# An RWKV-6 recurrence and a leaky-ReLU feed-forward on one Trainium2 core, rebuilt: tokens on partitions, three K tiles, 128-token blocks, a planned order

## The chip, the cores and the metric

The kernel runs on one core of one Trainium2 chip. The time is device microseconds of that core. The engines are named as in the profile: PE is TensorE's matmul, PEld its weight load, DVE is VectorE, ACT is ScalarE, POOL is GpSimd and SP is SyncE, which here only issues DMAs.

## The reference

Four batches of eight heads, 768 tokens, 48 elements a head; `r`, `k`, `v`, `w` are f32. A recurrence per head gives 384 values a token, and these go through a feed-forward with 2048 hidden units.

```python
for t in range(S):
    cur = np.einsum('bhd,bhe->bhde', u[None] * kt, vt)
    y[:, :, t] = np.einsum('bhd,bhde->bhe', rt, state + cur)
    state = wt[:, :, :, None] * state + np.einsum('bhd,bhe->bhde', kt, vt)
...
x = attn_out.transpose(0, 2, 1, 3).reshape(B * S, H * D)     # 3072 x 384
h = x @ w_in                                                 # 384 x 2048
g = np.maximum(0.01 * h, h)
out = g @ w_out                                              # 2048 x 384
```

The kernels do the recurrence in chunks of 128 tokens. Within a chunk the decays are products of `w`, so their logarithms are summed with a triangular matmul. `r` and `k` are multiplied by the exponentials of these sums, a masked 128 x 128 score matrix times `v` gives what tokens of one chunk give each other, a 48 x 48 state carries the rest from chunk to chunk, and `r*u*k` summed over a head gives the token's own term.

## The kernel before, in words

It loops over four batches and, in each, over six chunks of 128 tokens; after every third chunk comes a feed-forward block of 384 tokens (`mlp_block`). Only the tile framework orders the work: each engine takes its instructions in the order that the framework's scheduler has given them.

**Loading.** `w` comes as one transfer for a whole batch (L191), and its logarithm is taken in one ACT instruction per batch (L197). `r`, `k` and `v` come by chunk (L212, L216, L220) into f32 tiles with heads padded to 64; POOL clears the padding first (L209 to L211). The feed-forward weights are loaded with a cast to bf16 by POOL's own DMA queue after the first chunk (L127 to L135).

**A chunk.** One matmul gives the suffix sums of the log decays (L227), ACT takes the exponential (L235) and POOL multiplies it with `k` for the state (`dk`, L239). POOL makes `r*u*k` (L241, L245), DVE sums it by head (L249) and scales `v` with it (`vsc`, L251). Then four head pairs: `r` and `k` are transposed in f32 on PE (L261, L269), prefix sums of the decay come transposed from a third matmul (L277), ACT takes their exponentials (L285), DVE multiplies (L290), PE makes two score blocks (L296), DVE masks them (L303). Per head, PE adds the masked scores times `v` (L313), the own term through an identity matmul (L317), the old state's part (L325) and the new state's sum (L332). ACT or DVE copies y, which stands with d_model on partitions, into `xT` (L185), and DVE updates the state (L344). `xT` holds d_model in four K tiles of a head pair each, 112 rows with a gap.

**A feed-forward block.** For each of 16 tiles of 128 hidden units, four matmuls of 384 columns (L149) fill a PSUM tile `hp`, ACT casts it to bf16 (`hs`, L157), and DVE makes max(0.01 h, h) from both (`gt`, L159). Then 3 x 16 matmuls of 384 columns (L171) make three output tiles, copied by ACT (L179) and stored by SP (L180). `hp` and the output tile `op` share two buffers.

Of the kernel before, what the change touches and what calls it, by code (L numbers as in the profile page):

```python
# [8 lines left out]
F32 = mybir.dt.float32  # L9
BF16 = mybir.dt.bfloat16  # L10
AF = mybir.ActivationFunctionType
ALU = mybir.AluOpType
AX = mybir.AxisListType


@with_exitstack
def kernel(
# [11 lines left out]
    nc = tc.nc  # L29
    B, H, S, D = r.shape  # L30
    L = 128
    assert S % L == 0
    C = S // L
    assert H % 2 == 0
    NPAIR = H // 2
    assert D <= 48
    NH = H * D
    NT = NPAIR
    KROWS = 64 + D
    FF = moe_w_in.shape[1]  # L40
    assert FF % 128 == 0
    NFT = FF // 128
    NOUT = moe_w_out.shape[1]
    NTOK = B * S
    MB = 384
    assert S % MB == 0, "sequence must be multiple of mlp block"
    MBC = MB // L

    const = ctx.enter_context(tc.tile_pool(name="const", bufs=1))
    wpool = ctx.enter_context(tc.tile_pool(name="wpool", bufs=1))  # L50
    xtpool = ctx.enter_context(tc.tile_pool(name="xtpool", bufs=1))
    wbpool = ctx.enter_context(tc.tile_pool(name="wbpool", bufs=2))
    natpool = ctx.enter_context(tc.tile_pool(name="natpool", bufs=5))
    slabpool = ctx.enter_context(tc.tile_pool(name="slabpool", bufs=3))
    pairpool = ctx.enter_context(tc.tile_pool(name="pairpool", bufs=8))
    statepool = ctx.enter_context(tc.tile_pool(name="statepool", bufs=2))
    mlppool = ctx.enter_context(tc.tile_pool(name="mlppool", bufs=3))
    gtpool = ctx.enter_context(tc.tile_pool(name="gtpool", bufs=20))
    psum = ctx.enter_context(tc.tile_pool(name="psum", bufs=1, space=bass.MemoryType.PSUM))
    psum2 = ctx.enter_context(tc.tile_pool(name="psum2", bufs=2, space=bass.MemoryType.PSUM))  # L60

    ident_f = const.tile([128, 128], F32, name="ident_f")
    make_identity(nc, ident_f)
    ident_b = const.tile([128, 128], BF16, name="ident_b")
    make_identity(nc, ident_b)

    tcomb = const.tile([128, 256], BF16, name="tcomb")
    nc.gpsimd.memset(tcomb[:, 0:128], 1.0)
    nc.gpsimd.affine_select(
        out=tcomb[:, 0:128],  # L70
        in_=tcomb[:, 0:128],
        compare_op=ALU.is_gt,
        fill=0.0,
        base=0,
        pattern=[[1, 128]],
        channel_multiplier=-1,
    )
    nc.gpsimd.memset(tcomb[:, 128:256], -1.0)
    nc.gpsimd.affine_select(
        out=tcomb[:, 128:256],  # L80
        in_=tcomb[:, 128:256],
        compare_op=ALU.is_ge,
        fill=0.0,
        base=0,
        pattern=[[1, 128]],
        channel_multiplier=-1,
    )
    tsu = const.tile([128, 128], BF16, name="tsu")
    nc.gpsimd.memset(tsu[:], 1.0)
    nc.gpsimd.affine_select(  # L90
        out=tsu[:],
        in_=tsu[:],
        compare_op=ALU.is_gt,
        fill=0.0,
        base=0,
        pattern=[[-1, 128]],
        channel_multiplier=1,
    )
    maskb = const.tile([128, 128], BF16, name="maskb")
    nc.gpsimd.memset(maskb[:], 1.0)  # L100
    nc.gpsimd.affine_select(
        out=maskb[:],
        in_=maskb[:],
        compare_op=ALU.is_gt,
        fill=0.0,
        base=0,
        pattern=[[1, 128]],
        channel_multiplier=-1,
    )
    ukb = const.tile([128, H, D], F32, name="ukb")  # L110
    nc.sync.dma_start(
        out=ukb[:],
        in_=u.rearrange("h d -> (h d)")
        .partition_broadcast(128)
        .rearrange("p (h d) -> p h d", h=H),
    )

    w_in_b = wpool.tile([128, NT, FF], BF16, name="w_in_b")
    w_out_b = wpool.tile([128, NFT, NOUT], BF16, name="w_out_b")
    weights_loaded = [False]  # L120

    def load_weights():
        if weights_loaded[0]:
            return
        weights_loaded[0] = True
        for t in range(NT):
            nc.gpsimd.memset(w_in_b[32:64, t, :], 0.0)  # L127
            nc.gpsimd.dma_start(
                out=w_in_b[0:D, t, :], in_=moe_w_in[(2 * t) * D : (2 * t + 1) * D, :]
            )  # L130
            nc.gpsimd.dma_start(
                out=w_in_b[64 : 64 + D, t, :],
                in_=moe_w_in[(2 * t + 1) * D : (2 * t + 2) * D, :],
            )
        nc.gpsimd.dma_start(  # L135
            out=w_out_b[:], in_=moe_w_out.rearrange("(t p) n -> p t n", p=128)
        )

    xT = xtpool.tile([128, NT, NTOK], BF16, name="xT")

    state_tiles: list = [None] * NPAIR

    def mlp_block(q: int):
        T0 = q * MB
        gts = []
        for j in range(NFT):
            hp = psum2.tile([128, MB], F32, name="hp", tag="hpop")
            for t in range(NT):
                nc.tensor.matmul(  # L149
                    hp[:],  # L150
                    lhsT=w_in_b[0:KROWS, t, j * 128 : (j + 1) * 128],
                    rhs=xT[0:KROWS, t, T0 : T0 + MB],
                    start=(t == 0),
                    stop=(t == NT - 1),
                )
            hs = gtpool.tile([128, MB], BF16, name="hs", tag="hs", bufs=4)
            nc.any.tensor_copy(out=hs[:], in_=hp[:])  # L157
            gt = gtpool.tile([128, MB], BF16, name="gt", tag="gt")
            nc.vector.scalar_tensor_tensor(  # L159
                out=gt[:],  # L160
                in0=hp[:],
                scalar=0.01,
                in1=hs[:],
                op0=ALU.mult,
                op1=ALU.max,
            )
            gts.append(gt)
        for tsub in range(MB // 128):
            op = psum2.tile([128, NOUT], F32, name="op", tag="hpop")
            for j in range(NFT):  # L170
                nc.tensor.matmul(  # L171
                    op[:],
                    lhsT=gts[j][:, tsub * 128 : (tsub + 1) * 128],
                    rhs=w_out_b[:, j, :],
                    start=(j == 0),
                    stop=(j == NFT - 1),
                )
            osb = mlppool.tile([128, NOUT], F32, name="osb", tag="osb")
            nc.any.tensor_copy(out=osb[:], in_=op[:])  # L179
            nc.sync.dma_start(  # L180
                out=out[T0 + tsub * 128 : T0 + (tsub + 1) * 128, :], in_=osb[:]
            )

    def xt_copy(src_ap: bass.AP, p: int, col0: int):
        nc.any.tensor_copy(out=xT[:, p, col0 : col0 + L], in_=src_ap)  # L185

    for b in range(B):
        for p in range(NPAIR):
            state_tiles[p] = None
        w_nat = wbpool.tile([128, H * C, D], F32, name="w_nat", tag="w_nat")  # L190
        nc.sync.dma_start(  # L191
            out=w_nat[:],
            in_=w[b].rearrange("h (c p) d -> p (h c) d", p=128),
        )
        lw = wbpool.tile([128, C, H, 64], BF16, name="lw", tag="lw")
        nc.gpsimd.memset(lw[:, :, :, D:64], 0.0)
        nc.scalar.activation(  # L197
            out=lw[:, :, :, 0:D].rearrange("p c h d -> p h c d"),
            in_=w_nat[:].rearrange("p (h c) d -> p h c d", h=H),
            func=AF.Ln,  # L200
        )
        for c in range(C):
            t0 = c * L
            col0 = b * S + t0
            lw_c = lw[:, c, :, :]
            nat_rf = natpool.tile([128, H, 64], F32, name="nat_rf", tag="nat_rf")
            nat_kf = natpool.tile([128, H, 64], F32, name="nat_kf", tag="nat_kf")
            nat_vf = natpool.tile([128, H, 64], F32, name="nat_vf", tag="nat_vf")
            nc.gpsimd.memset(nat_rf[:, :, D:64], 0.0)  # L209
            nc.gpsimd.memset(nat_kf[:, :, D:64], 0.0)  # L210
            nc.gpsimd.memset(nat_vf[:, :, D:64], 0.0)  # L211
            nc.sync.dma_start(  # L212
                out=nat_rf[:, :, 0:D],
                in_=r[b, :, t0 : t0 + L, :].rearrange("h p d -> p h d"),
            )
            nc.sync.dma_start(  # L216
                out=nat_kf[:, :, 0:D],
                in_=k[b, :, t0 : t0 + L, :].rearrange("h p d -> p h d"),
            )
            nc.sync.dma_start(  # L220
                out=nat_vf[:, :, 0:D],
                in_=v[b, :, t0 : t0 + L, :].rearrange("h p d -> p h d"),
            )
# [129 lines left out]
            if b == 0 and c == 0:  # L353
                load_weights()
# [33 lines left out]
```

## Time and profile before

| | |
|---|---|
| time, median of 2 runs | 391.64 us (390.86 to 392.42) |
| span in the profile | 385.2 us, 6034 instructions |
| HBM read and written | 25.36 MB and 4.72 MB |
| mean granted TensorE clock | 0.978 |
| L149 hp, 512 matmuls, start to start in a run of eight | 162.5 ns |
| L157 ACT cast of hp, 122 | 480 ns mean |
| L159 DVE max, 128 | 554 ns mean |
| L285 ACT exponential of 256 columns, 96 | 384 ns mean |
| L303 DVE mask of 128 columns, 192 | 286 ns mean |
| L241 POOL product of 384 columns, 24 | 1051 ns mean |
| table loads on ACT, 8 | 1283 ns each |

The busy totals say what share of the span an engine had work. In a row of tenths, each digit is a fortieth of the span. Busy times of PE are modelled: a matmul's end lies past the start of the next, so PE's price is best read from starts. A group's idle column says what the engine waited for just before it; an engine that isn't the bound may wait at no cost.

### The profile page before, as it was taken

How to read it: one execution, taken by the hardware profiler on the slowest of the kernel's cores; microseconds unless marked ns; L12 is line 12 of the kernel's file. 1: busy time of each engine (PE TensorE's matmuls, PEld its weight loads, DVE VectorE, ACT ScalarE, POOL GpSimd, SP SyncE). 2: the span in 40 equal slices, each digit the busy share in tenths (PEclk: the TensorE clock that was granted, in tenths of full speed). 3: DMA queues.
4: the chain of work that ended last, by engine and by line, in shares of the span. 5: the costliest groups of instructions: out<-in, count | busy, mean ns of one | idle time of the engine just before them, and what ended most of it. 6: DMA issues, size and time to landing. Idle time of an engine off the chain costs nothing.

```text
span 385.2 us, 6034 instructions
## 1 busy us (share of the span) xinstructions
PE 337.2 (88%) x2136; PEld 187.8 (49%) x2136; DVE 219.8 (57%) x662; ACT 161.4 (42%) x382; POOL 107.8 (28%) x177
## 2 busy tenths in 40 slices
PE   0455169999999999999999999999999999999886
PEld 0232034455555555556555555555555655555343
DVE  0434045448656884767568837675588457724450
ACT  1535012343375633454486433542375235512341
POOL 5893055141152431234144303331331011000000
PEclk9999999999987999999999999999999999998699
DMA  7999999131532225212323233222220100010001
GB/s 159 176 205 227 217 166 167 15 64 20 128 57 54 39 57 115 48 21 53 96 42 58 57 93 60 41 43 82 43 41 3 62 2 0 2 61 3 0 0 63
DMA packets 87295, 27.33 MB, mean 71 GB/s; under 512 B 75489, under 2 KB 86881, under 8 KB 87265
## 3 DMA queue, kind: packets, MB, share of 16 engines
q1 hardware_dynamic: 84688, 23.80, 31.9%
q0 software_dynamic: 2576, 3.15, 4.8%
q8 instruction: 17, 0.28, 0.3%
q14 instruction: 14, 0.11, 0.1%
HBM read 25.36 MB, written 4.72 MB: 78 GB/s over the span
## 4 chain that ended last, share of the span: by engine, by line
PE 79%; SPq 7%; DMA 5%; DVE 5%; ACT 2%; issue 1%
PE hp L149 24%; PE op L171 16%; PE ytsu L325 7%; PE ytsu L332 6%; PE ytsu L313 6%; PE trcs L261 5%; PE mt L296 4%; DMA w_nat<-in_w_dram 4%; SPq L212 4%; PE trcs L269 3%; PE trcs L277 3%; PE ytsu L317 3%; DVE gt L159 2%; SPq L191 2%; PE esu_ps L227 1%; DVE vsc L251 1%
## 5 line engine op out<-in xcount | busy, mean ns | idle before, releaser
L149 PE MATMUL hp<-xT,w_in_b 112*128 112x384 bf16 x512 | 112.5, 347 | 8.6 <-DVE gt L159 7.0
L159 DVE SCALAR_TENSOR_TENSOR gt<-hp,hs 128x384 bf16<-128x384 f32 x128 | 70.1, 554 | 29.6 <-ACT hs L157 28.3
L157 ACT CAST hs<-hp 128x384 bf16<-128x384 f32 x122 | 58.3, 480 | 53.7 <-PE hp L149 52.3
L149 PEld LDWEIGHTS <-w_in_b 112*128 112x128 bf16 x512 | 50.2, 102 | 41.6 <-issue 18.7
L303 DVE TENSOR_TENSOR mtm<-mt,maskb 128x128 bf16<-128x128 f32 x192 | 51.2, 286 | 27.8 <-PE mt L296 27.1
L171 PE MATMUL op<-w_out_b,gt 128*128 128x384 bf16 x384 | 63.7, 326 | 0.4 <-DVE gt L159 0.4
L285 ACT ACTIVATE ef<-trcs 128x256 f32<-128x256 f32 x96 | 36.2, 384 | 47.6 <-PE trcs L277 45.3
L171 PEld LDWEIGHTS <-gt 128*128 128x128 bf16 x384 | 37.6, 98 | 25.0 <-issue 0.6
L313 PE MATMUL ytsu<-mtm,nat_v 128*64 128x128 bf16 x192 | 47.0, 255 | 1.3 <-DVE mtm L303 1.3
L239 POOL TENSOR_TENSOR dk<-nat_kf,esu 128x512 bf16<-128x512 f32 x24 | 27.8, 1157 | 71.7 <-ACT esu L235 71.3
L185 ACT CAST xT<-ytsu 128x128 bf16<-128x128 f32 x88 | 23.4, 266 | 51.0 <-PE ytsu L332 50.3
L261 PE MATMUL trcs<-ident_f,nat_rf 128*128 128x128 f32 x96 | 32.5, 338 | 13.1 <-DMA nat_rf<-in_r_dram 9.7
L317 PE MATMUL ytsu<-ident_b,vsc 128*64 128x128 bf16 x192 | 43.6, 236 | 0.0
L290 DVE TENSOR_TENSOR rka<-trcs,ef 128x256 bf16<-128x256 f32 x96 | 39.0, 408 | 4.7 <-ACT ef L285 4.7
L332 PE MATMUL ytsu<-nat_v,dk 128*64 128x64 bf16 x192 | 40.8, 222 | 0.0
L325 PE MATMUL ytsu<-rka,s_new 64*64 64x128 bf16 x160 | 40.3, 252 | 0.0
L313 PEld LDWEIGHTS <-nat_v 128*64 128x64 bf16 x192 | 20.2, 110 | 36.8 <-issue 28.8
L296 PE MATMUL mt<-rka 48*128 48x128 bf16 x192 | 28.4, 236 | 8.0 <-DVE rka L290 8.0
L241 POOL TENSOR_TENSOR t<-nat_rf,ukb 128x384 f32<-128x384 f32 x24 | 25.2, 1051 | 32.4 <-DMA nat_rf<-in_r_dram 32.3
L179 ACT COPY osb<-op 128x384 f32<-128x384 f32 x24 | 11.5, 479 | 52.5 <-PE op L171 52.5
L344 DVE SCALAR_TENSOR_TENSOR s_new<-s_new,atot,ytsu 128x64 bf16<-128x64 bf16 x80 | 21.9, 277 | 18.8 <-ACT xT L185 18.2
L251 DVE TENSOR_TENSOR vsc<-nat_vf,diag 128x512 bf16<-128x512 f32 x24 | 22.9, 956 | 14.3 <-PE ytsu L317 14.2
(47 smaller groups left out, 323.0 us busy)
## 6 DMA issues: line engine op xcount, KB each, us to landing
nat_rf<-in_r_dram SPq DMA_DIRECT2D x24, 192.0 KB, 3.2
nat_kf<-in_k_dram SPq DMA_DIRECT2D x24, 192.0 KB, 3.6
nat_vf<-in_v_dram SPq DMA_DIRECT2D x24, 192.0 KB, 2.9
out_dram<-osb SPq DMA_DIRECT2D x24, 192.0 KB, 1.9
w_in_b<-in_moe_w_in_dram POOLq DMA_DIRECT2D x8, 192.0 KB, 8.9
w_out_b<-in_moe_w_out_dram POOLq DMA_DIRECT2D x1, 1536.0 KB, 20.6
ukb<-in_u_dram SPq DMA_DIRECT2D x1, 192.0 KB, 3.6
w_nat<-in_w_dram SPq DMA_DIRECT2D x4, 0.2 KB, 16.3
```

Source lines behind the costliest of these rows:

```text
L149: nc.tensor.matmul(hp[:], lhsT=w_in_b[0:KROWS, t, j * 128 : (j + 1) * 128], rhs=xT[0:KROWS, t, T0 : T0 + MB], start=(t == 0), stop=(t == N ...
L157: nc.any.tensor_copy(out=hs[:], in_=hp[:])
L159: nc.vector.scalar_tensor_tensor(out=gt[:], in0=hp[:], scalar=0.01, in1=hs[:], op0=ALU.mult, op1=ALU.max,)
L171: nc.tensor.matmul(op[:], lhsT=gts[j][:, tsub * 128 : (tsub + 1) * 128], rhs=w_out_b[:, j, :], start=(j == 0), stop=(j == NFT - 1),)
L261: nc.tensor.matmul(trcs[:, 0:128], lhsT=nat_rf[:, hA : hA + 2, :].rearrange("p h d -> p (h d)"), rhs=ident_f[:], is_transpose=True, start= ...
L290: nc.vector.tensor_tensor(out=rka[:], in0=trcs[:, 0:256], in1=ef[:, 0:256], op=ALU.mult)
L296: nc.tensor.matmul(mt[:], lhsT=rka[r0 : r0 + D, 128:256], rhs=rka[r0 : r0 + D, 0:128], start=True, stop=True,)
L303: nc.vector.tensor_tensor(out=mtm[:, hi * 128 : (hi + 1) * 128], in0=mt[:], in1=maskb[:], op=ALU.mult,)
L313: nc.tensor.matmul(yap, lhsT=nat_v[:, hd, :], rhs=mtm[:, hi * 128 : (hi + 1) * 128], start=True, stop=False,)
L317: nc.tensor.matmul(yap, lhsT=vsc[:, hd, :], rhs=ident_b[:], start=False, stop=(s_prev is None),)
L325: nc.tensor.matmul(yap, lhsT=s_prev[r0 : r0 + 64, :], rhs=rka[r0 : r0 + 64, 0:128], start=False, stop=True,)
L332: nc.tensor.matmul(ytsu[r0 : r0 + 64, 128:192], lhsT=dk[:, hd, :], rhs=nat_v[:, hd, :], start=True, stop=True,)
```

## The change

The kernel is written anew. What it does and what for:

- **Tokens stand on partitions** through the decay, so `r`, `k`, `w`, `v` need no padding memsets, and the decay is one suffix sum for all heads; `r` and `k` are multiplied by exponentials of it and of its negative, and are transposed afterwards, in bf16.
- **d_model is 3 K tiles of 128** rather than 4 of 112, for the up projection; y is transposed on PE into them.
- **Feed-forward blocks are 128 tokens.** Four hidden tiles share one PSUM bank, and one ACT Prelu of 512 columns replaces the cast and the max.
- **The own term** is added by DVE when y leaves PSUM, not by an identity matmul.
- **Weights** come in f32 on the SP queue in eight loads of 786 KB and are cast half on DVE, half on ACT.
- **The order** on all engines is planned. Every piece of work becomes a step with an engine, a cost, its dependencies and a priority; `Plan.order` runs a list schedule in which each engine takes the ready step of lowest priority number, and the steps are then issued in the order of their planned starts. A DMA takes its planned wire time after the earlier ones and 1.7 us more. A `Ring` hands out buffers in turn and adds the old users of a buffer to the new user's dependencies.
- **Priorities**: ten per chunk for attention, 1000 and up for feed-forward matmuls, 5 for a Prelu; the up projection of block n alternates with the down projection of block n-1. The Ln of chunk n waits for the first up projection of chunk n-4 (`LEAD`), the loads of chunk n for the sums of chunk n-5 (`AHEAD`). `w_in` is loaded behind chunk 0 and `w_out` behind chunk 2.

The new branches for `APE` and `NPE` below 24 (totals and transposes by DMA) are not taken, as there are 24 chunks. The diff, cut to its core:

```diff
+    APE = 24
+    NPE = 24
+    LEAD = 4
+    AHEAD = 5
+
+    WEIGHTS = [(1, 4)] * 4 + [(3, 24)] * 4
+    blocks = [1] * NCH
...
+    in_r = ring("in", 11, [128, 1536], F32)
+    lw_r = ring("lw", 3, [128, H, 64], BF16)
...
+    g_r = ring("g", 4, [128, NJ, max(blocks) * L], BF16)
...
+    hp_r = ring("hp", 2, [128, 512], F32, psum)
+    op_r = ring("op", 1, [128, DM], F32, psum)
+    cp_r = ring("cp", 1, [128, 512], F32, psum)
+    se_r = ring("se", 1, [128, NP, 128], F32, psum)
+    so_r = ring("so", 1, [128, NP, 128], F32, psum)
+    yp_r = ring("yp", 1, [128, H, D], F32, psum)
+    pp_r = ring("pp", 1, [128, NP, 2, D], F32, psum)
...
+        nc.scalar.preload_act_table_set("natural_log_exp_and_others")
...
+            ld = step("SP", 0.45, load, pri, writes=[st], wire=2.2)
...
+            for i, (before, pri) in enumerate(WEIGHTS):
+                if n == before:
+                    weight_steps(i % NQ, i // NQ, pri)
...
+                    "SP", 0.45, load, P0, writes=[slot], wire=0.97,
+                    deps=[cums[n - AHEAD]] if n >= AHEAD else []))
...
+            def cum(cp=cp, lw=lw, tot=(not first and a_pe)):
                 nc.tensor.matmul(
...
+                    cp.t[:, 0:DM].rearrange("p (h d) -> p h d", h=H), lhsT=trev[:],
+                    rhs=lw.t[:, :, 0:D], start=True, stop=True, skip_group_check=True)
+                if tot:
+                    for p in range(NP):
+                        nc.tensor.matmul(
+                            cp.t[:, DM + p : DM + p + 1],
+                            lhsT=lw.t[:, 2 * p : 2 * p + 2, :].rearrange("p h d -> p (h d)"),
+                            rhs=ones[:], start=True, stop=True, skip_group_check=True)
...
+                def tpose(rk=rk, trv=trv):
+                    for g in range(2 * NP):
+                        nc.tensor.transpose(
+                            trv[:, g, :],
+                            rk.t[:, g // NP, 2 * (g % NP) : 2 * (g % NP) + 2, :].rearrange("p h d -> p (h d)"),
+                            ident[:])
...
+            s_ru = step(
+                "POOL", 1.05,
+                lambda ru=ru, rn=rn: nc.gpsimd.tensor_tensor(out=ru.t[:], in0=rn.t, in1=ubv, op=ALU.mult),
+                P0 + 2, reads=[rn], writes=[ru], deps=[rl, u_ld])
...
+            def scores(rkT=rkT, se=se, so=so):
+                for p in range(NP):
+                    for par, sc in enumerate((se, so)):
+                        q0 = 64 * par
+                        nc.tensor.matmul(
+                            sc.t[:, p, :], lhsT=rkT.t[q0 : q0 + D, NP + p, :],
+                            rhs=rkT.t[q0 : q0 + D, p, :], start=True, stop=True, skip_group_check=True)
+
+            s_sc = step("PE", 0.42, scores, P0 + 1, reads=[rkT], writes=[se, so], deps=s_T)
...
+                def sums(pp=pp, rk=rk, vb=vb):
+                    for p in range(NP):
+                        nc.tensor.matmul(
+                            pp.t[:, p, :, :],
+                            lhsT=rk.t[:, 1, 2 * p : 2 * p + 2, :].rearrange("p h d -> p (h d)"),
+                            rhs=vb.t[:, 2 * p : 2 * p + 2, :],
+                            start=True, stop=True, skip_group_check=True)
...
+                    "DVE", dve(NP * 128, 120),
+                    lambda m=m, sc=sc, par=par: nc.vector.tensor_tensor(
+                        out=m.t[:, par, :, :], in0=sc.t[:],
+                        in1=maskb[:].unsqueeze(1).to_broadcast([128, NP, 128]), op=ALU.mult),
...
+            def intra(m=m, vb=vb, yp=yp, rkT=rkT, sb=sb):
+                if sb is not None:
+                    for p in range(NP):
+                        nc.tensor.matmul(
+                            yp.t[:, 2 * p : 2 * p + 2, :], lhsT=rkT.t[:, p, :],
+                            rhs=sb.t[:, p, :, :], start=(p == 0), stop=False, skip_group_check=True)
...
+                        yp.t[:, h, :], lhsT=m.t[:, h % 2, h // 2, :], rhs=vb.t[:, h, :],
...
+                tr = so_r.take()
+                trv = tr.t[:].bitcast(BF16).rearrange("p a (b t) -> p (a b) t", b=2)
+
+                def typose(y=y, trv=trv):
+                    for g in range(KT):
+                        nc.tensor.transpose(
+                            trv[:, g, :],
+                            y.t[:].rearrange("p h d -> p (h d)")[:, g * 128 : (g + 1) * 128], ident[:])
...
+                def up(hp, j=j, J=J, N=N, c0=c0):
+                    for a in range(J):
+                        for t in range(KT):
+                            nc.tensor.matmul(
+                                hp.t[:, a * N : (a + 1) * N],
+                                lhsT=w_in_b[:, t, (j + a) * 128 : (j + a + 1) * 128],
+                                rhs=xT[:, t, c0 : c0 + N], start=(a == 0 and t == 0),
+                                stop=(t == KT - 1), skip_group_check=True)
...
+                    "ACT", act(J * N),
+                    lambda hp=hp, g=g, j=j, J=J, N=N: nc.scalar.activation(
+                        out=g.t[:, j : j + J, 0:N],
+                        in_=hp.t[:, 0 : J * N].rearrange("p (a n) -> p a n", a=J),
+                        func=AF.Prelu, alpha=0.01),
...
+                def down(op=op, g=g, q=q, off=off):
+                    for j in range(q * NJ // 4, (q + 1) * NJ // 4):
                         nc.tensor.matmul(
...
+                            op.t[:], lhsT=g.t[:, j, off : off + 128], rhs=w_out_b[:, j, :],
+                            start=(j == 0), stop=(j == NJ - 1))
...
+            if n >= LEAD:
+                plan.deps[lns[n]].append(up_done[n - LEAD])
```

## The prediction, made before the changed kernel ran

> **What bounds it now.** I read the busy totals first, then the tenths by slice, then busy time by stretch, and last TensorE's list of instructions in order of time inside one steady stretch.
>
> ```profile
> PE 337.2 (88%) x2136; PEld 187.8 (49%) x2136; DVE 219.8 (57%) x662; ACT 161.4 (42%) x382; POOL 107.8 (28%) x177
> ...
> PE   0455169999999999999999999999999999999886
> ...
> PEclk9999999999987999999999999999999999998699
> DMA  7999999131532225212323233222220100010001
> GB/s 159 176 205 227 217 166 167 15 64 20 128 57 54 39 57 115 48 21 53 96 42 58 57 93 60 41 43 82 43 41 3 62 2 0 2 61 3 0 0 63
> ```
>
> A slice is 385.2/40 = 9.6 us. In the first six PE is at 0 to 5 tenths while the DMA row is at 7 to 9: that start waits for data. From the seventh slice PE is at 9 until the last three, so the middle is TensorE's. The stretches say it in numbers (busy us and counts of PE, PEld, DVE, ACT, POOL, then clock, DMA share, GB/s):
>
> ```profile
> 0.00:20.00 20.00, 5.45 (x28) 2.91 (x28) 4.97 (x11) 7.37 (x11) 14.10 (x30) 1.00 1.00 169
> 20.00:35.00 15.00, 5.89 (x33) 3.52 (x32) 4.59 (x14) 7.33 (x13) 11.68 (x27) 1.00 1.13 211
> 35.00:60.00 25.00, 12.92 (x63) 6.55 (x62) 7.71 (x28) 3.56 (x11) 5.68 (x9) 1.00 1.21 196
> ...
> 120.00:200.00 80.00, 78.34 (x545) 45.00 (x543) 56.39 (x170) 41.26 (x99) 23.89 (x37) 1.00 0.29 61
> 200.00:280.00 80.00, 78.39 (x545) 45.21 (x544) 54.90 (x167) 35.99 (x97) 23.16 (x37) 1.00 0.28 59
> ```
>
> 24.3 us of PE work in the first 60, then 98% busy. A matmul's modelled end overlaps the next, so I price PE by starts. One head pair (start us, duration, engine, line):
>
> ```profile
> 295.52 0.24 PE L313 MATMUL ytsu<-mtm,nat_v 128*64 128x128 bf16 x1
> 295.60 0.22 PE L317 MATMUL ytsu<-ident_b,vsc 128*64 128x128 bf16 x1
> 295.75 0.24 PE L325 MATMUL ytsu<-rka,s_new 64*64 64x128 bf16 x1
> 295.92 0.22 PE L332 MATMUL ytsu<-nat_v,dk 128*64 128x64 bf16 x1
> ...
> 296.47 0.23 PE L296 MATMUL mt<-rka 48*128 48x128 bf16 x2
> 296.63 0.33 PE L261 MATMUL trcs<-ident_f,nat_rf 128*128 128x128 f32 x1
> 296.80 0.27 PE L269 MATMUL trcs<-ident_f,nat_kf 128*128 128x128 f32 x1
> 296.91 0.27 PE L277 MATMUL trcs<-tcomb,lw 128*128 128x256 bf16 x1
> 297.01 7.96 PE L171 MATMUL op<-w_out_b,gt 128*128 128x384 bf16 x48
> ```
>
> From 295.52 to 297.01 is 1.49 us for a pair. The 48 matmuls of L171 take (7.96 - 0.16)/48 = 162.5 ns each; eight of L149 on the chain of waits take 1.30 us, the same. So PE's work now is 512 x 0.1625 = 83 us up, 384 x 0.1625 = 62 us down, 96 pairs x 1.49 = 143 us and 24 x 0.21 = 5 us of L227 (280.92 to 281.14 in the same list): 294 us, of which 24 fit into the slow start.
>
> **What the Trainium skill says.** "TensorE: Matmul & The Clock Gate", section "Back-to-back issue gap", gives N/2.4 + 2.5 ns for an isolated matmul; at N=384 this is 162.5 ns, exactly the trace's pace with a new weight load each time. For N=128 it gives 56 ns by that formula and about 81 ns sustained with a weight load for each. No row here has a bf16 N=128 stream with 128 weight columns over 128 rows; the nearest, L296 (48 rows), makes two in 0.16 us, 80 ns each. "ScalarE: Activation LUTs", section "Table sets: the hidden batching unit", says Exp and Ln share one set and that cheap functions such as Relu and Copy are in every set; it does not settle Prelu. A load costs 1283 ns there and 1283 ns in each of the eight here. "SBUF — State Buffer", section "Who interferes with whom", says that a VectorE instruction with two SBUF inputs blocks against a GpSimd one that reads SBUF. L251 agrees: 0.69 us when POOL is quiet, 1.67 us at 125.97, mean 956 ns.
>
> **PE, by parts.** All per chunk of 128 tokens, 24 chunks.
> Up projection: three full K tiles in place of four of 112 rows, 128 tokens in place of 384: 16 x 3 = 48 matmuls of N=128. Each needs its own weight load beside only 128 columns. Bounds 56 and 81 ns; I take 65, because the load is wholly hidden at 384 columns (162.5) and behind L277's 256 columns (next start 0.10 us later), so part of it should hide here too: 3.1 us (2.7 to 3.9). Before: 83/24 = 3.5.
> Down projection: unchanged, 16 x 0.1625 = 2.6 us.
> Attention: the suffix-sum matmul (N=384, 0.16), 4 column totals, 8 bf16 transposes of decayed r and k, 8 scores, 4 state sums, 4 products with the state, 8 with the mask, 3 transposes of y: 39 small matmuls with 128 weight columns. At 70 ns, between the two bounds and the L296 pace: 39 x 0.07 + 0.16 = 2.9 us (2.3 to 3.3). Before: 4 x 1.49 + 0.21 = 6.2. The saving is here: fp32 transposes, the identity matmul that added the diagonal, the second cumulative sum and the 64-column matmuls go.
> Sum 3.1 + 2.6 + 2.9 = 8.6 us a chunk (7.6 to 9.8), 206 us in all (182 to 235), against 294.
>
> **The other engines.** DVE: from L303 (128 elements from PSUM, 286 ns), L290 (256, 408) and L159 (384, 554), a PSUM source of 512 is about 650 ns. A chunk has the add to the sums, y and the output copy (3 x 0.55), one half transposed copy (0.65), two masks (1.3), two state updates (2 x 0.35, interpolated), the reduce (L249, 0.54), the bf16 v (L225 scaled, 0.45) and two SBUF products (L251 scaled to 384, 0.55 free, 0.8 with the port taken): 6.4 to 6.9 us. It stays under 8.6. ACT: from L285 (256, 384 ns), L179 (384, 479) and L235 (512, 596): Ln, two Exps and the xT copy 4 x 0.5, one 512 copy, four Prelus 4 x 0.6, the total's Exp 0.2: 5.2 us. Prelu takes over from L157 and L159 together (480 + 554 ns each time, in series before a buffer is free), so PE's waits for L159 (7.0 us on hp) should go. Seven of eight table loads go if Prelu is in the preloaded set: 9 us of ACT, hidden. POOL: three products at 1.05 (L241) and two half ones at 0.5: 4.2 us. The memsets and casting DMAs of L127 to L135 and L209 to L211 leave POOL, at no gain to the end: POOL is 28% busy. Weight casts move to DVE and ACT, about 8 each of under 1 us, inside the start while both are idle.
>
> **The start.** Loads of 192 KB move at about 160 GB/s (slice 1): 1.2 us each, 4.9 us a chunk. The weights, 6.3 MB of f32, moved best in slices 3 to 5 at 205 to 227 GB/s, so 14 to 15 us for each matrix. In one SP queue chunk 0 lands near 8 us, w_in near 23, chunks 1 and 2 near 33, w_out near 48, chunk 3 near 53. The first down projection can't finish before 48. Up to then PE can do three chunks' attention and up projection, 3 x 6.0 = 18 us. The planner's own wire times (2.2 us for a 786 KB weight load) are 1.6 times faster than these rates, so its fixed PE order will hold instructions in front of data that has not come; that loss lies inside these 48 us. w_nat's whole-batch load (16.3 us to land) is gone; the start still shrinks by little, because the weights stand in the one queue.
>
> **New waits.** Ln of chunk n waits for the first up projection of chunk n-4; behind it on ACT stand Exps and Prelus, and PE waits for those. The four-chunk lead covers it. Loads of chunk n wait on SP for the sums of n-5; stores of outputs queue there too, but 5 x about 1 us of SP time a chunk fits in 8.6. The score banks se and so also take the transposes, so scores of n+1 wait for the xT copy of n: scores 0.6, masks 1.3, y 0.6, add 0.55, transpose 0.25, copy 0.5, and about 0.2 us to pass from engine to engine six times: 5.0 us, under 8.6 with 3.6 to spare for queueing.
>
> **Sum.** 48 + (206 - 18) = 236, plus 4 us of tail (the last down matmul started at 373.69 + 48 x 0.1625 = 381.5 of 385.2 before), plus 391.6 - 385.2 = 6 us outside the span: **246 us**. I add nothing for steady stalls, since PE is 98% busy in such stretches now and the hp buffers stay double.
>
> **Rivals.** *The attention loop bounds* (18%): if in-order queues cost each of the loop's ten hops half a neighbour (0.5 us), the loop is 10.2 us. Chunk 3's xT near 62, twenty more at 10.2 is 266, plus one up and down projection 6, tail 4, outside 6: 282 us. For it: single banks, DVE 75 to 80% loaded, the shared port. Against: the 3.6 us of slack a chunk. *The weight loads hide wholly* (14%): 56 to 58 ns each, 7.6 us a chunk, 182 in all; weights at 227 GB/s end near 44 with 15 us of PE done: 44 + 167 + 10 = 221, and with a few us of stalls 224. For it: 162.5 shows the formula exact; against: the 80 ns of L296. *Prelu outside the set* (6%): four Prelus between Exps make about 8 loads a chunk, 8 x 1.28 + 5.2 = 15.5 us on ACT, 372 in all, plus 18 for the start and 10: 400 us, slower than now, and more with the drain that the skill adds to a switch. For it: the page does not settle it. Against: an explicit preload, and its word on cheap functions. The forecast has 62%.
>
> **The numbers.** The range runs from 224 to 282, the two nearer rivals, and leaves out the far ends of each and the table case. Faster by over 2% is all but the table case and a failing start: 0.93; within 2% 0.02; slower 0.05.
>
> **What would show it.** Right: PE at 9 tenths from about slice 9, starts of the up projection 60 to 70 ns apart, attention near 2.9 us of PE a chunk, one table load, DVE under 80%. Up starts of 81 ns put the time near 260. Wrong: PE waiting for masks, y or xT in the middle means the loop; many table loads mean the last rival; FF outputs starting long after 48 us means the start was mis-sized.

## The result, and the profile after

The changed kernel takes **222.79 us** (222.69 to 222.89, two runs) against 391.64 us: a ratio of 0.568 with a 95% interval of 0.564 to 0.572. The forecast was 246.0 us with a range of 224 to 282: the direction was right, and the time lies just below the range.

The page of the kernel after, the lines that answer to those shown of before:

```profile
span 220.8 us, 6043 instructions
...
PE 186.3 (84%) x2448; PEld 144.2 (65%) x2448; DVE 155.6 (70%) x299; ACT 118.7 (54%) x245; POOL 98.6 (45%) x125
...
PE   0446679887979998949899999999999999999983
...
DVE  6653995589999999996878876977967565620021
...
PEclk9999559999999999988999999999999999999999
DMA  7999999999999999939089267846010110001101
GB/s 130 318 355 184 297 355 165 179 193 189 200 185 216 188 210 201 200 76 181 18 162 177 61 122 147 174 98 128 36 39 2 37 39 36 3 36 39 39 36 71
```

A slice is 5.5 us now. PE's busy time fell from 337.2 to 186.3 us with 312 more matmuls. PE stands at 9 throughout only from the 21st slice; DVE does from the tenth to the eighteenth. Slices two, three, five and six show 297 to 355 GB/s, the weights. Two slices (22 to 33 us) have half the clock.

The busy time by stretch says which engine is full when (busy us and counts of PE, PEld, DVE, ACT, POOL, then clock, DMA share, GB/s):

```profile
0.00:30.00 30.00, 13.59 (x131) 10.58 (x132) 19.66 (x42) 13.80 (x25) 13.91 (x25) 0.88 1.01 267
30.00:60.00 30.00, 26.40 (x329) 19.96 (x327) 23.70 (x45) 18.64 (x39) 16.07 (x19) 0.95 1.11 201
60.00:100.00 40.00, 34.10 (x489) 26.47 (x489) 38.81 (x72) 21.61 (x49) 25.78 (x31) 0.97 0.97 181
100.00:190.00 90.00, 85.48 (x1192) 66.77 (x1188) 67.81 (x133) 53.27 (x116) 42.32 (x52) 0.99 0.43 88
190.00:217.50 27.50, 26.69 (x318) 20.42 (x315) 5.15 (x11) 11.40 (x20) 0.49 (x1) 1.00 0.11 38
```

From 60 to 100 us DVE is 97% busy: there the attention part, which the plan's priorities let run ahead of the feed-forward part, stands at DVE. From 100 us on PE is the bound at 95 to 97%. The longest stall between 60 and 100 us shows how DVE holds PE up:

```profile
94.34 3.28 DVE L323 CAST vb<-in 128x384 bf16<-128x384 f32 x3
97.55 0.55 DVE L537 TENSOR_TENSOR y<-yp,vs 128x384 bf16<-128x384 f32 x1
98.15 0.50 PE L547 MATMUL so<-ident,y 128*128 128x128 bf16 x3 [2.62 <-DVE y L537]
```

In DVE's order three casts of v stand ahead of the y that PE needs (its matmuls end at 93.69), and beside a busy POOL they take 1.1 us each, where the cast at 98.81 takes 0.34. So DVE's busy time holds waiting too.

PE's list in order of time, inside a steady stretch (start us, duration, line; a group's pace is read from start to start):

```profile
129.58 0.83 PE L579 MATMUL hp<-xT,w_in_b 128*128 128x128 bf16 x12
130.71 0.23 PE L471 MATMUL se<-rkT 48*128 48x128 bf16 x1 [0.30 <-DVE s L510]
...
131.04 0.82 PE L631 MATMUL op<-w_out_b,g 128*128 128x384 bf16 x4
131.70 1.50 PE L579 MATMUL hp<-xT,w_in_b 128*128 128x128 bf16 x24
...
133.69 0.33 PE L522 MATMUL yp<-sb,rkT 128*128 128x96 bf16 x4
133.86 0.36 PE L526 MATMUL yp<-vb,m 128*128 128x48 bf16 x8
134.06 0.32 PE L332 MATMUL cp<-lw,trev 128*128 128x384 bf16 x1
...
134.97 0.83 PE L579 MATMUL hp<-xT,w_in_b 128*128 128x128 bf16 x12
135.64 0.33 PE L547 MATMUL so<-ident,y 128*128 128x128 bf16 x3
135.81 0.81 PE L631 MATMUL op<-w_out_b,g 128*128 128x384 bf16 x4
```

Twelve up matmuls take 135.64 - 134.97 = 0.67 us, **55.8 ns** each. Eight masked products (L526) take 134.06 - 133.86 = 0.20 us, **25 ns** each, and four products with the state (L522) 0.17 us, 42.5 ns. Four down matmuls take 0.65 us, 162.5 ns, as before.

### The profile page after: what moved, and what is told of

The parts are those of the page before. It is cut to its first block, busy times and chain, and to the rows that moved or that the text cites. A ratio compares the mean times of both kernels' runs of the same rounds, so it can differ in the third digit from the quotient of the medians.

```text
span 220.8 us, 6043 instructions
## 1 busy us (share of the span) xinstructions
PE 186.3 (84%) x2448; PEld 144.2 (65%) x2448; DVE 155.6 (70%) x299; ACT 118.7 (54%) x245; POOL 98.6 (45%) x125
## 4 chain that ended last, share of the span: by engine, by line
PE 49%; DVE 23%; DMA 8%; ACT 7%; issue 7%; SPq 2%; POOL 2%; DVEq 0%; ACTq 0%; POOLq 0%
PE hp L579 19%; PE op L631 18%; DVE rk L373 4%; DVE ci L347 3%; DMA in<-in_moe_w_in_dram 3%; DVE m L494 3%; PE se L385 3%; DVE s L510 3%; PE se L471 3%; DMA in<-in_w_dram 2%; DVE y L537 2%; ACT er L354 2%; DMA in<-in_r_dram 2%; DVE vb L323 2%; PE so L547 2%
## 5 line engine op out<-in xcount | busy, mean ns | idle before, releaser
L579 PE MATMUL hp<-xT,w_in_b 128*128 128x128 bf16 x1152 | 81.0, 225 | 0.8 <-ACT xT L553 0.8
L613 ACT ACTIVATE g<-hp 128x512 bf16<-128x512 f32 x96 | 57.4, 598 | 39.4 <-PE hp L579 38.5
L631 PE MATMUL op<-w_out_b,g 128*128 128x384 bf16 x384 | 77.8, 329 | 0.6 <-DVE o L642 0.6
L579 PEld LDWEIGHTS <-w_in_b 128*128 128x128 bf16 x1152 | 72.5, 101 | 7.5 <-issue 1.2
L631 PEld LDWEIGHTS <-g 128*128 128x128 bf16 x384 | 33.1, 98 | 16.5 <-issue 1.8
L462 POOL TENSOR_TENSOR sb<-s,a 64x192 bf16<-64x192 f32 x40 | 25.6, 639 | 28.8 <-ACT a L435 24.9
L411 POOL TENSOR_TENSOR ru<-in,ub 128x384 f32<-128x384 f32 x24 | 24.7, 1033 | 25.0 <-DMA in<-in_r_dram 21.1
L423 POOL TENSOR_TENSOR vs<-in,dg 128x384 f32<-128x384 f32 x24 | 20.0, 834 | 35.2 <-DVE dg L419 11.4
L642 DVE COPY o<-op 128x384 f32<-128x384 f32 x24 | 13.3, 555 | 23.2 <-PE op L631 22.8
L415 POOL TENSOR_TENSOR ru<-ru,in 128x384 f32<-128x384 f32 x24 | 25.7, 1074 | 1.5
L385 PE MATMUL se<-ident,rk 128*128 128x128 bf16 x192 | 18.3, 230 | 7.8 <-DVE rk L367 3.9
L367 DVE TENSOR_TENSOR rk<-in,er 128x384 bf16<-128x384 f32 x24 | 18.2, 759 | 2.3 <-ACT er L354 2.1
L373 DVE TENSOR_TENSOR rk<-in,ek 128x384 bf16<-128x384 f32 x24 | 18.0, 750 | 1.2 <-ACT ek L360 1.1
```

The source lines that it names most:

```text
L367: lambda rk=rk, rn=rn, er=er: nc.vector.tensor_tensor(out=rk.t[:, 0, :, 0:D], in0=rn.t, in1=er.t[:, :, 0:D], op=ALU.mult),
L373: lambda rk=rk, kn=kn, ek=ek: nc.vector.tensor_tensor(out=rk.t[:, 1, :, 0:D], in0=kn.t, in1=ek.t[:], op=ALU.mult),
L385: nc.tensor.transpose(trv[:, g, :], rk.t[:, g // NP, 2 * (g % NP) : 2 * (g % NP) + 2, :].rearrange("p h d -> p (h d)"), ident[:])
L411: lambda ru=ru, rn=rn: nc.gpsimd.tensor_tensor(out=ru.t[:], in0=rn.t, in1=ubv, op=ALU.mult),
L415: lambda ru=ru, kn=kn: nc.gpsimd.tensor_tensor(out=ru.t[:], in0=ru.t[:], in1=kn.t, op=ALU.mult),
L423: lambda vs=vs, vn=vn, dg=dg: nc.gpsimd.tensor_tensor(out=vs.t[:], in0=vn.t, in1=dg.t[:].unsqueeze(2).to_broadcast([128, H, D]), op=ALU.mult),
```

## The experiments

The kernel before ran beside each batch, at 386.59 us for the first four runs, 390.60 for the next four and 391.66 for the last four; the kernel after was not repeated. Differences in us are against its 222.79. On the first chip the kernel before is 1.3% quicker than in the result, so a ratio to the kernel before is given as well; against the result's 0.568 it puts the first four runs 3 to 4 us higher than the plain difference does.

**Does the width of the weights cost, or the number of matmuls?** Each masked product is split into two of 64 weight columns:

```diff
-                    nc.tensor.matmul(
-                        yp.t[:, h, :], lhsT=m.t[:, h % 2, h // 2, :], rhs=vb.t[:, h, :],
...
+                    for q0 in (0, 64):
+                        nc.tensor.matmul(
+                            yp.t[q0 : q0 + 64, h, :], lhsT=m.t[:, h % 2, h // 2, q0 : q0 + 64],
+                            rhs=vb.t[:, h, :],
...
```

> Each of the eight masked-score matmuls of a chunk (L526, 128 weight columns, 25 ns apart in the changed kernel) is made as two with 64 weight columns each. If the width of the weight load is what made the small matmuls cheap after the change and dear before it (L313 to L332, 64 weight columns, about 100 ns each), a chunk gains 16 x 0.10 - 0.20 = 1.4 us of PE, 33 us in all, less what hides where PE waits anyway: 240 to 255 us. If only the number of matmuls counts, 16 x 0.025 - 0.20 = 0.2 us a chunk: 225 to 228 us.

Measured 227.12 us (226.23 to 229.14), ratio 0.5885 (0.5834 to 0.5935). That is 4.3 us more (8 by the ratios) and lies near "only the number", far from the other range. PE's list of this kernel:

```profile
135.88 0.33 PE L522 MATMUL yp<-sb,rkT 128*128 128x96 bf16 x4
136.14 0.43 PE L527 MATMUL yp<-vb,m 128*64 128x48 bf16 x16
136.51 0.34 PE L332 MATMUL cp<-lw,trev 128*128 128x384 bf16 x1
```

Sixteen take 0.37 us where eight took 0.20. The single starts in the trace show the two halves of a pair 4 ns apart and pairs about 32 ns apart; but the first half starts 0.136 us after the last L522, against 0.043 in the kernel after, and L332 starts 0.122 us after the last half, against 0.025. So in the kernel after a masked product with 128 fresh weight columns takes no more than 25 ns, and here about 0.09 us goes into each change from one shape of array tile to another, once in and once out. "TensorEngine Tiling (Array Packing)", section "Key Properties", says that such a change drains TensorE and that different tiles work in parallel; the two gaps and the 4 ns agree with it.

**Does the weights' start set the end?** The weights come by POOL's casting queue again, without the casts on DVE and ACT:

```diff
-            st = in_r.take()
...
-            ld = step("SP", 0.45, load, pri, writes=[st], wire=2.2)
...
+            made = [step("POOL", 0.6, load, pri, wire=2.2)]
```

(`load` writes the bf16 tile directly.)

> The weights come by POOL's casting DMAs again, straight into the bf16 tiles, instead of f32 loads on the SP queue with casts on DVE and ACT. If the start was mis-sized because such loads move at the 205 to 227 GB/s of the kernel before while plain ones reach 318 to 355, w_in and w_out are ready some 10 us later and the time is 228 to 236 us. If the start is hidden under the attention that DVE limits afterwards, it is 219 to 226 us.

Measured 223.60 us (223.29 to 223.86), ratio 0.5786 (0.5753 to 0.5819): 0.8 us more, or 4 by the ratios. The page's GB/s row, its casting queue (packets, MB, share) and its weight issues (KB each, us to landing):

```profile
GB/s 132 152 191 187 185 146 191 189 173 195 179 211 184 192 197 234 132 133 176 53 177 109 136 114 124 143 139 136 37 38 8 30 38 35 9 30 38 38 50 57
...
q0 software_dynamic: 3712, 3.15, 8.7%
...
w_in_b<-in_moe_w_in_dram POOLq DMA_DIRECT2D x4, 384.0 KB, 11.4
w_out_b<-in_moe_w_out_dram POOLq DMA_DIRECT2D x4, 384.0 KB, 20.1
```

The kernel after has in their place

```profile
in<-in_moe_w_in_dram SPq DMA_DIRECT2D x4, 768.0 KB, 8.2
in<-in_moe_w_out_dram SPq DMA_DIRECT2D x4, 768.0 KB, 8.7
```

The two matrices are 6.29 MB in f32, and the casting queue counts 3.15 MB: the profile counts a casting load by the bf16 bytes that it writes. So the 146 to 191 GB/s of this row can't be set against the 297 to 355 of the kernel after. By the packets in the traces, all weights move between 7.5 and 32.7 us here and between 5.6 and 34.2 us in the kernel after, there with a pause from 16.0 to 23.0. Casting didn't make them late as a whole. What changed is the order: the first up projection starts 3.5 us later (18.3 against 14.8) and the second 5.4 later (36.0 against 30.6), but the first down projection starts earlier (24.0 against 31.9). At the end the last up matmul starts at 212.1 against 211.2. So a late start of the up projection hardly reached the end here; how much a late arrival of all weights would cost isn't shown, and the casts are gone from DVE and ACT at the same time.

**How much of PE's work reaches the end?** The middle K tile of the up projection is counted twice, 384 more matmuls or 21.4 us of PE:

```diff
-                        for t in range(KT):
+                        for t in (0, 1, 1, 2):
```

> The up projection adds the middle K tile twice, so 384 more matmuls of 128 columns with their weight loads; the output differs by that. At 55.8 ns each this is 21.4 us. If PE sets the pace from the start on, 241 to 245 us. If DVE sets it up to about 100 us and PE afterwards, only the later 14 blocks pay, 16 x 14 x 0.056 = 12.5 us: 232 to 238 us. If the loop through the score banks sets it, 222 to 227 us.

Measured 237.68 us (234.48 to 237.96), ratio 0.6153 (0.6111 to 0.6195): 14.9 us more, the second range, so 0.7 of the added PE work comes through (18.4 us, 0.86, by the ratios). PE is not the bound everywhere, and still most of its work counts.

**And of DVE's?** The own term is left out: no products on POOL, no reduce, and y is copied rather than added:

```diff
...
-                lambda y=y, yp=yp, vs=vs: nc.vector.tensor_tensor(
-                    out=y.t[:], in0=yp.t[:], in1=vs.t[:], op=ALU.add),
+                lambda y=y, yp=yp: nc.vector.tensor_copy(out=y.t[:], in_=yp.t[:]),
```

> Leaves out the own term r*u*k times v (L411, L415, L419, L423), so y is copied out of PSUM without it. POOL then works for the states alone and DVE loses the reduce (0.54) and the waits on the shared port (0.2 in each of L367 and L373, 0.27 in L323): 1.2 us a chunk. If DVE and its port limit the stretch from 36 to 100 us, some nine chunks gain about 1 us each: 210 to 215 us. If PE limits all along, 220 to 223 us.

Measured 216.90 us (215.54 to 216.93), ratio 0.5604 (0.5567 to 0.5642): 5.9 us less, between the two (3 us less by the ratios). From 60 to 100 us DVE is busy 29.3 us instead of 38.8, and POOL 5.0 instead of 25.8, so the wait for the shared port goes with it. The product of r (L367), first in the kernel after and then in this one:

```profile
L367 DVE TENSOR_TENSOR rk<-in,er 128x384 bf16<-128x384 f32 x24 | 18.2, 759 | 2.3 <-ACT er L354 2.1
```

```profile
L367 DVE TENSOR_TENSOR rk<-in,er 128x384 bf16<-128x384 f32 x24 | 13.3, 554 | 1.9 <-ACT er L354 1.8
```

The product of k falls from 750 to 571 ns and the cast of v from 607 to 384. How much of the gain is this waiting and how much the reduce that is gone was not tried apart.

**The cheap operation in the old kernel.** The kernel before with one Prelu in place of cast and max:

```diff
-            hs = gtpool.tile([128, MB], BF16, name="hs", tag="hs", bufs=4)
-            nc.any.tensor_copy(out=hs[:], in_=hp[:])
...
-            nc.vector.scalar_tensor_tensor(
...
+            nc.scalar.activation(out=gt[:], in_=hp[:], func=AF.Prelu, alpha=0.01)
```

> The kernel before with one part of the change alone: ACT's Prelu writes gt from hp, in place of L157 and L159. If the two in series held PE only where nothing else was there to do, it gains the 7 us that hp waits for L159, above all in the last block, where two hidden tiles take 1.97 us instead of 1.3: 374 to 384 us. If Prelu lies outside the set of Exp, table loads grow by tens and it is slower than 391 us.

Measured 454.89 us (454.29 to 457.34), a ratio of 1.175 (1.164 to 1.185) to the kernel before: slower, and not for the reason expected of a slower one. There are eight table loads as before, so Prelu needs none. The page's clock row and two stretches:

```profile
PEclk9999999995599557965589656985589755995589
```

```profile
120.00:135.00 15.00, 15.00 (x82) 8.29 (x82) 4.75 (x12) 8.29 (x18) 1.52 (x4) 0.89 0.14 27
150.00:160.00 10.00, 10.00 (x48) 5.07 (x46) 4.52 (x18) 3.30 (x9) 3.21 (x6) 0.50 0.21 40
```

From 120 to 135 us its PE list has almost only up and down projections, from 150 to 160 almost only attention, and there the granted clock is half. The framework's scheduler now puts the up projection in runs of 56 matmuls, where the kernel before has mostly runs of four or eight; stretches of attention alone longer than 3 us add up to 157 us after the start, in the kernel before to 41. "TensorE: Matmul & The Clock Gate", Part 1, says that the array runs at half rate when it has been idle; here it falls while the page calls PE 100% busy. Why these small matmuls lower it was not tried apart. What follows is only that this edit changed the order as well, so it isn't a price of Prelu.

**Prelu alone, in the new kernel.** Cast on ACT and maximum on DVE come back:

```diff
-                    "ACT", act(J * N),
...
-                        func=AF.Prelu, alpha=0.01),
+                    "ACT", act(J * N),
+                    lambda hp=hp, hs=hs: nc.scalar.copy(out=hs.t[:], in_=hp.t[:]),
...
+                    "DVE", dve(J * N, 120),
+                    lambda hp=hp, hs=hs, g=g, j=j, J=J, N=N: nc.vector.scalar_tensor_tensor(
...
```

> The changed kernel with the cast on ACT and the max on DVE again (512 columns each), planned with their costs. DVE gains 4 x 0.66 us a chunk and comes to 6.5 + 2.6 = 9.1 us, above PE's 7.0. If DVE then sets the pace, 24 x 9.1 plus a start of about 15 is 233 to 245 us. If PE still does, 222 to 228 us.

Measured 231.04 us (229.97 to 231.42), ratio 0.5951 (0.5908 to 0.5993): 8.2 us more, between the two. DVE is busy 201.0 us (88%), and from 100 to 190 us 86.7 of 90, where PE falls from 85.5 to 82.6. Prelu is worth 8 us in this kernel, and it takes 45 us off DVE.

**The order alone.** The same operations, but issued in the order in which they are written, with loads two chunks ahead:

```diff
+        self.slot.append(max(0, c - 4) if eng == "SP" and c % 2 == 0 else c)
...
-        for i in plan.order():
+        for i in sorted(range(len(plan.eng)), key=lambda i: (plan.slot[i], i)):
```

> The same steps in a plain order: attention of chunk n, then the up and down projections of the second chunk before it, loads two chunks ahead. If the gain came from cheaper matmuls alone and the order matters little, 225 to 245 us. If the list schedule hides the chain of one chunk's attention (about 6.4 us from transposes to xT, of which PE works 1.8), a chunk takes up to 6.4 + 5.3 = 11.7 us and the time is 270 to 310 us.

Measured 398.84 us (398.72 to 398.88), a ratio of 1.028 (1.021 to 1.035) to the kernel before: both expectations missed, and all of the gain is gone with this order. Its page:

```profile
PE 256.6 (65%) x2448; PEld 190.0 (48%) x2448; DVE 144.5 (36%) x299; ACT 123.2 (31%) x245; POOL 90.8 (23%) x125
...
PEclk9999858578588586785785866867767768668699
```

and PE's list over part of one chunk:

```profile
207.77 1.08 PE L389 MATMUL se<-ident,rk 128*128 128x128 bf16 x8 [1.82 <-DVE rk L371]
209.98 0.28 PE L475 MATMUL se<-rkT 48*128 48x128 bf16 x1 [1.14 <-ACT rkT L400]
...
211.76 0.48 PE L526 MATMUL yp<-sb,rkT 128*128 128x96 bf16 x4 [0.74 <-POOL sb L466]
...
213.57 1.49 PE L583 MATMUL hp<-xT,w_in_b 128*128 128x128 bf16 x12
214.85 1.49 PE L636 MATMUL op<-w_out_b,g 128*128 128x384 bf16 x4
...
218.35 0.83 PE L583 MATMUL hp<-xT,w_in_b 128*128 128x128 bf16 x12
219.02 0.81 PE L636 MATMUL op<-w_out_b,g 128*128 128x384 bf16 x4
```

PE waits at each link of the attention chain (the brackets), and after these gaps it runs at half clock: twelve up matmuls take 214.85 - 213.57 = 1.28 us at first, 107 ns each, and 219.02 - 218.35 = 0.67 us later. No engine is full.

**DVE again: one cast moved.** The bf16 copy of v goes from DVE to ACT (L323):

```diff
-                "DVE", dve(DM // 2),
-                lambda vb=vb, vn=vn: nc.vector.tensor_copy(out=vb.t[:], in_=vn.t),
+                "ACT", act(DM, 224),
+                lambda vb=vb, vn=vn: nc.scalar.copy(out=vb.t[:], in_=vn.t),
```

> The cast of v to bf16 (L323, 607 ns mean on DVE, of which part is waiting for POOL's hold of the shared port) moves to ACT at about 0.52 us. DVE falls by 14 us, ACT rises by 12 to 131 us. If DVE limits from 36 to 100 us, 212 to 218 us; if PE limits all along, 221 to 224 us.

Measured 219.41 us (218.1 to 220.5), ratio 0.5654 (0.5606 to 0.5702): 3.4 us less, between the two. By the ratios it is 1 us less, within their intervals, so this run alone shows little.

**The planner's costs.** Set to the durations measured in the kernel after, for instance:

```diff
-            return (src + n) / 960.0 + 0.03
+            return (src + n) / 960.0 - 0.05
...
-                "DVE", dve(DM // 2),
+                "DVE", 0.53,
...
-                s_up = step("PE", J * 3 * max(N / 2400 + 0.003, 0.06), lambda up=up, hp=hp: up(hp), pri,
+                s_up = step("PE", J * 3 * (N / 2400 + 0.003), lambda up=up, hp=hp: up(hp), pri,
```

> Only the planner's costs change, to what the changed kernel's trace shows: DVE steps 0.08 us cheaper, but 0.68 for L367 and L373 and 0.53 for L323 (they wait for the shared port), 0.35 for L392; PE 0.47 for the eight transposes, 0.38 for the y matmuls, 0.67 for twelve up matmuls, 0.18 for y's transposes; 0.62 for POOL's half products; 1.2 us of wire for a chunk load. If PE idles in the middle because its fixed order was planned on costs that DVE doesn't keep, some of the 17 us of PE idle between 30 and 100 us and of the 9 us between 100 and 190 go: 208 to 218 us. If the idle is set by DVE's own work and the loop through the score banks, the order hardly matters: 220 to 225 us.

Measured 221.00 us (219.30 to 222.41), ratio 0.5622 (0.5578 to 0.5666). That is the second range; true costs alone hardly help: DVE is still busy 38.3 of 40 us from 60 to 100.

**Two chunks ahead of the weights.** Two chunks' inputs are now loaded ahead of `w_in`, and four ahead of `w_out`, instead of one and three:

```diff
-    WEIGHTS = [(1, 4)] * 4 + [(3, 24)] * 4
+    WEIGHTS = [(2, 14)] * 4 + [(4, 34)] * 4
```

> Chunk 1 is loaded ahead of w_in and chunk 3 ahead of w_out, each one chunk earlier than in the changed kernel. If the attention's late start sets the first 100 us (chunk 1's w lands near 19 us, behind w_in), attention gains some 8 us and the time is 214 to 219 us, though the first up projection starts later. If w_in and w_out are what the start waits for, 224 to 230 us.

Measured 218.32 us (218.11 to 219.44), ratio 0.5574 (0.5543 to 0.5605), as expected. DVE is busy 14.2 of the first 20 us against 11.0, and the half clock of the start shrinks to one slice; which of the two brings the 4.5 us was not tried apart.

**Together.** Costs and the moved cast:

> The measured costs and the cast of v on ACT together. If both lift the same limit, DVE in the stretch to 100 us, they don't add up: about the better of the two alone, 212 to 219 us. If the planner's order and DVE's load are separate, about 205 to 212 us.

Measured 212.76 us (212.20 to 213.30), ratio 0.5426 (0.5395 to 0.5457): 10 us less, more than the 1.8 and 3.4 of the parts. The number lies at the edge of the first range, but its reason, that the two would not add up, failed. Its stretches:

```profile
60.00:100.00 40.00, 39.30 (x572) 31.10 (x570) 34.89 (x67) 29.62 (x66) 27.28 (x33) 0.97 1.05 199
100.00:190.00 90.00, 89.71 (x1295) 72.86 (x1295) 67.66 (x130) 62.01 (x132) 44.73 (x53) 1.00 0.42 88
```

With DVE at 87% instead of 97%, PE is busy 39.3 of 40 us from 60 to 100 (34.1 in the kernel after), and 89.7 of 90 from then to 190 (85.5). The moved cast alone brings DVE to 35.6 of 40 us but PE only to 36.1, and the costs alone leave DVE at 38.3 and bring PE to 36.1: both DVE's load and the planned order hold PE up there.

And with the earlier loads too:

> All three. If the start is limited by chunk 1's late data, this is the fastest of all, 203 to 212 us; if the weights are what the start waits for, it is slower than the one without the early loads.

Measured 211.82 us (210.71 to 212.80), ratio 0.5402 (0.5363 to 0.5441), just inside the first range. The lowest of all, but its interval overlaps that of the run without the earlier loads, so the earlier loads add nothing clear here.

## Why the prediction was right or wrong

**Right.** TensorE was the bound and remains it from 100 us on; the forecast came from its work and from the start. The down projection takes 162.5 ns. DVE has 155.6/24 = 6.5 us a chunk (foreseen 6.4 to 6.9), though that holds 8 us of weight casts and clearing, and it is 6.1 without them; ACT 4.9 (5.2), POOL 4.1 (4.2), the tail is 220.8 - 217.5 = 3.3 us (4). One table load is left, so the rival with Prelu outside the set falls. The attention loop doesn't bound at 10.2 us: xT copies come about every 6 us while DVE is full.

**Wrong: the prices in the PE sum.** The step that failed is the sum "3.1 + 2.6 + 2.9 = 8.6 us a chunk", 206 us in all. Two of its terms were mis-sized:

| | forecast | measured |
|---|---|---|
| up, 48 of N=128 | 65 ns, 75 us in all | 55.8 ns, 64 us |
| attention, a chunk | 39 x 70 ns + 0.16 = 2.9 us | about 1.7 us |
| attention in all | 70 us | 40 us |
| down | 62 us | 62 us |
| PE work | 206 us | 167 us |

Worked out from the counts and the starts, the 39 us split so. The first part is the weight load, which the forecast took to hide only in part. The trace has 55.8 ns over 1152 up matmuls with a fresh weight load each, 10 us less than forecast, and the same pace in place of 70 ns for the 888 small attention matmuls is 13 us. The second part, 13 us, is that most of these are narrower or run in pairs: the eleven transposes of a chunk have 128 columns (56 ns), the four state sums and the four products with the state 96 (42.5), the masked ones 48 and the totals 1 (25 each), and the eight scores run two at a time (about 0.33 us for all). The last 3 us are 48 matmuls that the first and last chunks of a batch don't have. The page "TensorE: Matmul & The Clock Gate", section "Back-to-back issue gap", gives the formula N/2.4 + 2.5 ns and about 81 ns as the sustained pace at N=128; the measurement decides for the formula. The 80 ns of L296, which the forecast leaned on, was a pair of another tile shape, between other shapes; the split of the masked products puts about 0.09 us on such a change, which is the likely cause.

The rival "the weight loads hide wholly" had this mechanism, and its 221 to 224 us are close to the time. That closeness is luck: its PE sum of 182 us is still 15 too high, and stalls that it put at a few us make up for it.

**Wrong the other way: "I add nothing for steady stalls".** With those prices PE is idle 50.7 us up to the end of its work at 217.5, half clock counted as idle: 23.5 before 30 us, 16.8 from 30 to 100, 9.0 from 100 to 190, 1.4 after. The forecast had 30 in the start and none later. DVE's 70% of the span hid its 97% from 60 to 100 us: products with two SBUF sources (L367, L373) take 0.76 and 0.75 us beside a busy POOL, near the prediction's upper price of 0.8, and 0.55 and 0.57 without the own term. That DVE is behind these stalls is supported by the runs together, not by one alone: less DVE work brings 3 to 6 and 1 to 3 us, more costs 8.2, and with both the cast moved and true costs PE's busy time there rises to 39.3 of 40 us.

**The start** was mis-sized too: the forecast has the first down projection end no earlier than 48 us, and its last four matmuls start at 37.3. The prediction divided the f32 bytes of the weights by the 205 to 227 GB/s of the kernel before, a row that counts casting loads at half of these bytes, as the run with casting loads shows. So the term was a misreading, not a slower kind of load. How much of it reaches the end isn't shown: PE's idle time before 30 us is 23.5, against the 30 of the forecast.

Summed: PE 166.8 - 206 = -39.2, idle +20.7, tail -0.7, outside the span 2.0 instead of 6: 246 - 23.2 = 222.8, as measured. The 6 us set the span of one execution against the times of others; in every run here whose time and span belong to one execution they differ by 1.7 to 2.0 us. So errors of both signs cancelled in part. The run with 21.4 us of added PE work says that such a change of PE's work reaches the end with 0.7 or more, so the 39 us of over-pricing are worth some 27 us or more by this estimate: enough for the miss.

**What the prediction didn't ask:** how much is the order's. The same operations in written order take 398.84 us, 176 us more than planned. The forecast assumed PE kept at work and at full clock; the plan does that for most of the span, and in the written order the fall of PE work from 294 to 167 us brings nothing. That is one other order; a better one without a planner was not tried.

## What to carry to other kernels

Price each small matmul at its own number of columns, and take the price from starts in a stretch of one tile shape; a row of another shape misleads. Before dividing bytes by a GB/s row, look up what its queue counts: a casting load stands there with the bytes that it writes. The cheaper operations paid here only with an order that keeps the bounding engine fed, so read the idle time between an engine's groups, and check each engine's share by stretch: 70% over the span can be 97% where it matters. Then move a little work off the engine that is full there, and let the plan know the true costs.

## What the runs showed of the hardware that was not expected

- Matmuls of 48 columns with 128 fresh weight columns each start 25 ns apart; with the weights split into 2 x 64 columns, both halves start 4 ns apart and the pairs about 32, but each change of tile shape costs about 0.09 us.
- The granted clock stood at 0.50 from 150 to 160 us in the kernel before with Prelu, although PE counted as busy all the time, with almost only attention's small matmuls; and up matmuls took 107 ns just after the gaps of the unplanned order.
- A casting load of the f32 weights is counted by its bf16 bytes (3.15 MB for 6.29). All weights were in by 32.7 us with casting loads on POOL's queue, by 34.2 us with plain ones on SP's.
- The cast of v took 384 ns in the mean with POOL almost idle and 607 beside a busy one; three of them in a row took 3.28 us.
